# Products of two groups in a row, the first rows of x in two halves, and a new table of thresholds, in a planned attention kernel

## The chip, the cores and the metric

The kernel runs on one core of a Trainium2 chip. The metric is the time of one execution on the device in microseconds (us), as the median of several runs. One further execution was taken by the hardware profiler; its rows are what the argument rests on. The engines are PE (matmuls; PEld is its weight load), DVE (vector), ACT (activations), POOL, and SP, which here only issues DMAs.

## What is computed

Two attention layers over 2048 positions of width 512 with 32 heads of width 16; their outputs stand side by side.

```python
# A: softmax attention
scores = jnp.einsum("bhqd,bhkd->bhqk", q, k) * Dh ** -0.5
p = _softmax(scores, axis=-1)
o = jnp.einsum("bhqk,bhkd->bhqd", p, v)        # then @ wo
# B: linear attention with learned features
phi_q = concat([softmax(pq), softmax(-pq)]); phi_k = concat([softmax(pk), softmax(-pk)])
kv = jnp.einsum("bhsf,bhsd->bhfd", phi_k, v); z = jnp.einsum("bhsf->bhf", phi_k)
o = (phi_q @ kv) / (phi_q @ z + 1e-6)          # then @ wo
return jnp.concatenate([a, b], axis=-1)
```

Nearly all of the time goes to A: 32 heads times 2048 by 2048 scores.

## The kernel before, in words

**Work of layer A.** Four heads form a group, and there are eight groups. A unit is one group with 128 or 256 queries; there are 73 units. For every unit the scores are made twice. First with the queries on the partitions: PE writes tiles of 128 by 512 scores into banks of PSUM (L971), and DVE reduces them to the maximum of each row (L1084), one bank by one instruction (a single) or two neighbouring banks by one (a pair). The negated maxima go by POOL and two DMAs (in the last four units by DVE and PE) into a spare row of QZ, the masked copy of the queries. Then with the keys on the partitions: PE makes the scores again, with the maximum already subtracted (L1234), and ACT takes the exponential of one or two banks into the ring pT of 34 slots (L1246). Last the product: for each 512 scores of the four heads PE multiplies pT with V (L1324, in `pv_run`), with V's extra column of ones giving the sums. When a unit is done, its product is evacuated to X, divided, and later multiplied with the output weights (`oproj`, L1419). A few units (11) move part of the maxima to ACT (a Relu, L1011) and one DVE instruction (L1078).

**Work beside it.** Projections of Q, K and V (L696, L710, L777), turning x by matmuls with the identity (L807), and all of layer B are cut into "jobs". A job takes a bank, runs its matmuls in pieces, and leaves the bank when an evacuation (`evac`, L560 on ACT or L563 on DVE) has copied it out.

**The planner.** The order on every engine is fixed when the program is built. An account of costs (`_Account`) plays the execution: it holds a clock `K.now`, the time at which each engine is free, and ready tasks. ACT, DVE, POOL and SP are asked in this order whether they are free and take the ready task of the lowest priority number; evacuations stand ahead of reductions and exponentials. For PE, `pick_pe` decides what comes next: a score tile for DVE (`d_fill`), one for ACT (`e_fill`), a product (`pv_run`), a piece of a job, or filler matmuls that keep PE's share of use up (`fill_mm`, L1854; also repeated scores). It decides by the leads `sd` and `se`, the work in time that stands ready for DVE and ACT, and by thresholds that are set anew every 60 us of the account (`T.set` with a row of `TH` over the defaults `TH0`):

- COL, INCOL: how large the smaller lead must be before products or jobs run, and before PE leaves them;
- SINGLE, ESINGLE: the lead below which a single is filled where no pair of banks is free; DCAP, ECAP: the largest lead up to which scores are filled; DBIAS and ZBIAS: who is served first;
- UA, RF, REPM, LHARD, LHI: how much use of PE is kept up by fillers and repeats;
- PV_START, PV_LOW, PVN: at how many free ring slots or ready groups products are wanted;
- BAL: an evacuation may go to DVE only if the work left for DVE, by the account, exceeds that for ACT by no more than BAL.

**The start.** Six idle matmuls (L368) run while the loads come. x comes in blocks of 128 rows on SP's queue: blocks 0 and 1, 2 and 3, 4 to 7, then the V weights, blocks 8 to 11, the rest of the K weights, blocks 12 to 15, the rest of the Q weights; the first K and Q weights come on ACT's queue. Blocks 0 to 3 are turned by 16 matmuls into banks 0 to 3 (L374), two idle matmuls follow, and DVE and ACT copy two banks of 512 columns each (L381, L383). DVE also copies the first K and Q weights into a padded form (L361). Then K and Q of the first group are projected for 512 positions (L710), and `first_qz` makes QZ of units 0, 1 and 2 from the Q bank (L734). The account begins at 7.6 us.

Of the kernel before, what the change touches and what calls it, by code (L numbers as in the profile page):

```python
# [213 lines left out]
def bass_concat_heads__softmax_full_mha__linear_kernel_hedgehog__prompt_kernel(  # L214
# [21 lines left out]
    with contextlib.ExitStack() as es:  # L236
# [5 lines left out]
        P = _Plan()  # L242
# [85 lines left out]
        def load_x(name, b0, b1):  # L328
            t_xs[name] = P.dma("sp", dsem("xs%d" % name), lambda e: e.dma_start(
                xs[:, b0:b1, :], A_x[0][128 * b0:128 * b1, :].rearrange("(b p) n -> p b n", p=128)))  # L330
# [5 lines left out]
        load_x(2, 4, 8)  # L336
# [27 lines left out]
        t_wqp = pad_copy(WQp, 0, t_wq0)  # L364
# [5 lines left out]

        pe_idle(6, [t_zmv, t_ones])
        for rb in range(4):
            for ct in range(4):
                t_turn = P.op("pe", lambda e, rb=rb, ct=ct: e.matmul(  # L374
                    PS[:, ct, 128 * rb:128 * rb + 128], xs[:, rb, ct * 128:ct * 128 + 128], ident[:, :],
                    start=True, stop=True), [t_xs[rb // 2], t_ident] if ct == 0 else [])
        pe_idle(2)
        t_x0 = []
        for ct in range(4):
            if ct % 2 == 0:  # L380
                t_x0.append(P.op("dve", lambda e, ct=ct: e.tensor_copy(xAT[:, ct, 0:512], PS[:, ct, :]), [t_turn]))  # L381
            else:
                t_x0.append(P.op("act", lambda e, ct=ct: e.activation(  # L383
                    xAT[:, ct, 0:512], PS[:, ct, :], ACT.Copy), [t_turn]))
# [17 lines left out]
        for r in range(4):  # L402
# [8 lines left out]
            {'SINGLE': 1.013, 'ESINGLE': 1.026, 'ZBIAS': 0.274, 'DBIAS': 0.27, 'ZREST': 0.238},  # L411
            {'SINGLE': 0.647, 'UA': 0.441, 'RF': 0.465, 'REPM': 0.115, 'PV_LOW': 6, 'DCAP': 2.442, 'ZBIAS': 0.207, 'BAL': 68.611},
            {'SINGLE': 1.013, 'UA': 0.408, 'REPM': 0.215, 'LHI': 0.119, 'DCAP': 1.302, 'ECAP': 1.815, 'ZBIAS': 0.315, 'DBIAS': 0.27, 'BAL': -28.613},
            {'SINGLE': 1.157, 'UA': 0.408, 'RF': 0.436, 'REPM': 0.215, 'LHI': 0.03, 'PV_START': 5, 'PV_LOW': 5, 'DCAP': 1.302, 'ECAP': 1.815, 'ZBIAS': 0.315, 'BAL': -28.613},
            {'SINGLE': 0.287, 'UA': 0.425, 'RF': 0.532, 'REPM': 0.196, 'LHARD': 0.35, 'LHI': 0.119, 'DCAP': 1.302, 'ECAP': 1.815, 'ZBIAS': 0.315, 'DBIAS': 0.27, 'BAL': -27.419},
            {'SINGLE': 1.157, 'UA': 0.408, 'RF': 0.436, 'REPM': 0.214, 'LHARD': 0.383, 'LHI': 0.03, 'PV_START': 5, 'PV_LOW': 5, 'PVN': 3, 'DCAP': 1.322, 'ECAP': 1.904, 'ZBIAS': 0.315, 'BAL': -27.335},
            {'COL': 0.708, 'SINGLE': 1.157, 'UA': 0.441, 'REPM': 0.196, 'LHI': 0.065, 'PVN': 3, 'DCAP': 2.495, 'ECAP': 1.461, 'ZBIAS': 0.315, 'DBIAS': 0.27, 'BAL': -27.419},
            {'ESINGLE': 1.165, 'RF': 0.62, 'REPM': 0.196, 'LHI': 0.065, 'ECAP': 1.185, 'ZBIAS': 0.049, 'DBIAS': 0.27, 'BAL': -27.419, 'ZREST': -0.23},
            {'ESINGLE': 1.2, 'RF': 0.62, 'REPM': 0.196, 'LHI': 0.122, 'ECAP': 1.185, 'ZBIAS': 0.049, 'DBIAS': 0.27, 'BAL': -27.419, 'ZREST': -0.23},
            {'COL': 0.63, 'INCOL': 0.753, 'ESINGLE': 1.097, 'RF': 0.436, 'REPM': 0.196, 'LHI': 0.079, 'JOBHOLD': 20.274, 'DCAP': 2.036, 'ECAP': 1.185, 'ZBIAS': 0.034, 'DBIAS': 0.314, 'BAL': -27.419, 'ZREST': -0.23},  # L420
            {'COL': 0.487, 'INCOL': 0.753, 'SINGLE': 0.633, 'ESINGLE': 1.097, 'RF': 0.596, 'REPM': 0.196, 'LHI': 0.079, 'JOBHOLD': 20.274, 'DCAP': 2.036, 'ECAP': 1.185, 'ZBIAS': 0.034, 'DBIAS': 0.334, 'BAL': -27.419, 'ZREST': -0.23},
            {'COL': 0.63, 'INCOL': 0.753, 'SINGLE': 0.663, 'ESINGLE': 1.097, 'UA': 0.458, 'RF': 0.676, 'REPM': 0.196, 'LHARD': 0.355, 'LHI': 0.246, 'JOBHOLD': 14.826, 'PV_START': 5, 'DCAP': 2.036, 'ECAP': 1.276, 'ZBIAS': 0.072, 'DBIAS': 0.278, 'BAL': -30.019, 'ZREST': -0.23},
            {'COL': 0.53, 'INCOL': 0.753, 'SINGLE': 0.674, 'ESINGLE': 1.097, 'UA': 0.442, 'RF': 0.67, 'REPM': 0.369, 'LHARD': 0.317, 'LHI': 0.259, 'JOBHOLD': 12.459, 'PV_START': 5, 'DCAP': 2.021, 'ECAP': 1.276, 'ZBIAS': 0.129, 'DBIAS': 0.278, 'BAL': -37.649, 'ZREST': -0.23},
            {'COL': 0.35, 'INCOL': 0.753, 'SINGLE': 0.749, 'ESINGLE': 1.097, 'UA': 0.433, 'RF': 0.67, 'REPM': 0.369, 'LHI': 0.259, 'JOBHOLD': 25, 'PV_START': 5, 'ECAP': 1.276, 'ZBIAS': 0.391, 'DBIAS': 0.278, 'BAL': -37.649, 'ZREST': -0.23},
            {'COL': 0.53, 'INCOL': 0.753, 'SINGLE': 0.749, 'ESINGLE': 1.097, 'UA': 0.442, 'RF': 0.67, 'REPM': 0.369, 'LHI': 0.259, 'JOBHOLD': 17.436, 'PV_START': 5, 'ECAP': 1.276, 'ZBIAS': 0.129, 'DBIAS': 0.278, 'BAL': -37.649, 'ZREST': -0.23},
            {'COL': 0.486, 'INCOL': 0.753, 'SINGLE': 0.638, 'ESINGLE': 1.097, 'UA': 0.442, 'RF': 0.67, 'REPM': 0.348, 'LHI': 0.259, 'JOBHOLD': 17.436, 'PV_START': 5, 'ECAP': 1.276, 'ZBIAS': 0.129, 'DBIAS': 0.278, 'BAL': -30.554, 'ZREST': -0.23},
            {'COL': 0.486, 'INCOL': 0.753, 'SINGLE': 0.638, 'ESINGLE': 1.097, 'UA': 0.442, 'RF': 0.67, 'REPM': 0.189, 'LHI': 0.259, 'JOBHOLD': 17.436, 'PV_START': 5, 'ECAP': 1.276, 'ZBIAS': 0.129, 'DBIAS': 0.278, 'BAL': -30.554, 'ZREST': -0.23},
            {'COL': 0.486, 'INCOL': 0.753, 'SINGLE': 0.735, 'ESINGLE': 1.057, 'UA': 0.442, 'RF': 0.648, 'REPM': 0.21, 'LHI': 0.234, 'JOBHOLD': 17.436, 'DCAP': 2.479, 'ECAP': 1.276, 'ZBIAS': 0.129, 'DBIAS': 0.278, 'BAL': -37.429, 'ZREST': -0.23},
            {'COL': 0.657, 'INCOL': 0.753, 'SINGLE': 0.735, 'ESINGLE': 1.057, 'UA': 0.442, 'RF': 0.648, 'REPM': 0.21, 'LHI': 0.234, 'JOBHOLD': 13.418, 'DCAP': 2.479, 'ECAP': 1.171, 'ZBIAS': 0.129, 'DBIAS': 0.278, 'BAL': -30.554, 'ZREST': -0.23},
            {'COL': 0.486, 'INCOL': 0.753, 'SINGLE': 0.933, 'ESINGLE': 1.057, 'UA': 0.442, 'RF': 0.61, 'REPM': 0.21, 'LHARD': 0.251, 'LHI': 0.285, 'JOBHOLD': 17.436, 'DCAP': 2.479, 'ECAP': 1.356, 'ZBIAS': 0.119, 'DBIAS': 0.111, 'BAL': -37.429, 'ZREST': -0.23},  # L430
        ]
        T = _Thresholds()
        I32 = mybir.dt.int32
        K = _Account(P)
        K.now = 7.6
        T.set(TH0, TH[:1])
        for i in range(1, int(1200 / SEG)):
            K.at(i * SEG, lambda i=i: T.set(TH0, TH[i:i + 1]))
        for e in K.free:
            K.free[e] = 7.6  # L440
        K.free["pool"] = 14.0

# [1638 lines left out]
```

## Time and profile before

| | us |
|---|---|
| three runs | 1199.12, 1202.8, 1205.19 |
| median | 1202.8 |
| profiled execution, its own time | 1199.05 |
| its span, from the first instruction to the last | 1197.3 |
| granted clock of PE, mean of the span | 0.999 |

In the rows of the profile a group is given as line, engine, operation, written tile <- read tiles, shapes and count, then busy time (overlaps of its own instructions counted once), mean duration in ns, and idle time of the engine before it with what ended it. A row of the timeline gives start, length, and the same names, with like instructions in a row put together. A row of the stages gives the busy time and count of the engines in one stretch of time.

### The profile page before, as it was taken

How to read it: one execution, taken by the hardware profiler on the slowest of the kernel's cores; microseconds unless marked ns; L12 is line 12 of the kernel's file. 1: busy time of each engine (PE TensorE's matmuls, PEld its weight loads, DVE VectorE, ACT ScalarE, POOL GpSimd, SP SyncE). 2: the span in 40 equal slices, each digit the busy share in tenths (PEclk: the TensorE clock that was granted, in tenths of full speed). 3: DMA queues.
4: the chain of work that ended last, by engine and by line, in shares of the span. 5: the costliest groups of instructions: out<-in, count | busy, mean ns of one | idle time of the engine just before them, and what ended most of it. 6: DMA issues, size and time to landing. Idle time of an engine off the chain costs nothing.

```text
span 1197.3 us, 32106 instructions
## 1 busy us (share of the span) xinstructions
PE 1117.4 (93%) x13025; PEld 468.9 (39%) x13025; DVE 1170.3 (98%) x1290; ACT 1149.8 (96%) x1891; POOL 821.8 (69%) x1636
## 2 busy tenths in 40 slices
PE   8998999998999999999999998999999998899998
PEld 3433333343334333333433333333333333345555
DVE  8999999999999999999999999999999999999995
ACT  5898999999999999999999999999999999999997
POOL 8511211227888888888787887888888888888860
PEclk9999999999999999999999999999999999999999
DMA  5011221210002001001000101121112111111120
GB/s 142 9 25 43 42 48 32 43 38 8 8 14 35 8 6 26 13 10 22 12 7 17 25 7 22 22 49 31 29 34 33 35 34 27 20 29 37 33 30 18
DMA packets 104119, 33.61 MB, mean 28 GB/s; under 512 B 86692, under 2 KB 103972, under 8 KB 103972
## 3 DMA queue, kind: packets, MB, share of 16 engines
q1 hardware_dynamic: 102916, 31.31, 13.4%
q8 instruction: 102, 1.67, 0.6%
q14 instruction: 45, 0.37, 0.1%
q10 hardware_dynamic: 1056, 0.26, 0.1%
HBM read 5.26 MB, written 4.19 MB: 8 GB/s over the span
## 4 chain that ended last, share of the span: by engine, by line
ACT 38%; DVE 33%; PE 23%; SPq 2%; issue 1%; POOL 1%; DMA 1%
ACT pT L1246 32%; DVE part L1084 32%; PE PS L1234 7%; PE PS L971 6%; PE PS L1324 5%; PE PS L1419 2%; ACT eB L1639 1%; ACT xAT L560 1%; PE PS L777 1%; ACT zS L1011 1%; ACT X L560 1%; SPq L1392 1%; ACT WQp L560 1%; POOL uB L1588 1%; PE PS L1563 0%
## 5 line engine op out<-in xcount | busy, mean ns | idle before, releaser
L1084 DVE TENSOR_REDUCE part<-PS 128x2 f32<-128x1024 f32 (+1 forms) x1118 | 1130.0, 1079 | 7.6 <-PE PS L971 5.2
L1246 ACT ACTIVATE pT<-PS 128x512 bf16<-128x512 f32 (+1 forms) x1573 | 1027.7, 797 | 21.3 <-PE PS L1234 17.9
L1234 PE MATMUL PS<-QZ,KT 64*128 64x256 bf16 (+1 forms) x4906 | 560.4, 259 | 40.9 <-ACT pT L1246 22.0
L971 PE MATMUL PS<-KT,QZ 64*128 64x512 bf16 x2139 | 484.5, 383 | 26.3 <-DVE part L1084 9.7
L1234 PEld LDWEIGHTS PS<-QZ,KT 64*128 64x128 bf16 x4906 | 245.5, 94 | 323.1 <-ACT pT L1246 161.4
L971 PEld LDWEIGHTS PS<-KT,QZ 64*128 64x128 bf16 x2139 | 126.2, 93 | 198.2 <-DVE part L1084 72.2
L1324 PE MATMUL PS<-pT,VP 128*17 128x256 bf16 (+1 forms) x4672 | 186.7, 261 | 0.9
L1403 POOL TENSOR_TENSOR QT<-X,Yd 128x256 bf16<-128x256 f32 (+1 forms) x70 | 46.8, 668 | 95.4 <-DMA Yd<-Yd 95.1
L1324 PEld LDWEIGHTS PS<-pT,VP 128*17 128x17 bf16 x4672 | 74.9, 88 | 95.2 <-issue 79.0
L1588 POOL TENSOR_TENSOR uB<-uB 128x256 f32<-128x256 f32 (+2 forms) x160 | 83.4, 522 | 10.1
L1591 POOL TENSOR_SCALAR uB<-uB 128x256 f32<-128x256 f32 (+2 forms) x128 | 82.6, 646 | 11.2
L1116 POOL TENSOR_TENSOR dm<-part 128x16 f32<-128x16 f32 (+1 forms) x66 | 15.7, 238 | 91.1 <-DVE part L1084 90.8
L915 POOL TENSOR_TENSOR QZ<-QT,mask 128x512 bf16<-128x512 bf16 (+1 forms) x70 | 65.9, 941 | 15.7 <-PE PS L1234 12.8
L1645 POOL TENSOR_TENSOR xAT<-eB 128x512 f32<-128x512 bf16 x32 | 36.9, 1152 | 40.8 <-ACT eB L1639 40.6
L1677 POOL TENSOR_TENSOR wA<-eB,rB 128x1024 bf16<-128x1024 bf16 x32 | 61.7, 1928 | 2.0
L560 ACT ACTIVATE xAT<-PS 128x512 f32<-128x512 f32 (+3 forms) x83 | 50.1, 617 | 4.4 <-PE PS L1443 2.9
L1648 POOL TENSOR_TENSOR xAT<-xAT 128x256 f32<-128x256 f32 x64 | 36.0, 563 | 5.0
L1563 PE MATMUL PS<-WKp,xBT 128*128 128x512 bf16 x128 | 36.4, 383 | 1.1 <-ACT pT L1246 0.5
L1639 ACT ACTIVATE eB<-uB 128x1024 bf16<-128x1024 f32 x32 | 36.0, 1124 | 0.0
L1419 PE MATMUL PS<-WOp,QT 128*128 128x512 bf16 x120 | 35.8, 384 | 0.1
L1588 POOL TENSOR_TENSOR uB<-xAT,mB 128x512 f32<-128x512 f32 x32 | 33.8, 1057 | 1.8
L1662 POOL TENSOR_TENSOR WQp<-rB,WQp 128x64 f32<-128x64 f32 x96 | 30.6, 319 | 6.4
(113 smaller groups left out, 752.4 us busy)
## 6 DMA issues: line engine op xcount, KB each, us to landing
out_dram<-xAT SPq DMA_DIRECT2D x31, 128.0 KB, 1.8
Yd<-Yd SPq DMA_DIRECT2D x220, 16.0 KB, 2.1
QT<-eB SPq DMA_DIRECT2D x60, 32.0 KB, 2.0
QZ<-mcols SPq DMA_DIRECT2D x110, 1.0 KB
pT<-in_A_x_dram SPq DMA_DIRECT2D x3, 512.0 KB, 7.5
KT<-eB SPq DMA_DIRECT2D x48, 32.0 KB, 2.0
mcols<-stage SPq DMA_TRANSPOSE x69, 2.2
Yd<-Yd SPq DMA_DIRECT2D x60, 8.0 KB, 1.9
```

The lines of the kernel that those rows point to most:

```text
L560: return P.op("act", lambda e: e.activation(dst, src, ACT.Copy), tk)
L915: "pool", lambda e: e.tensor_tensor(QZ[:, u % NQZ, :, 0:w], QT[:, g, q0:q0 + w].unsqueeze(1).broadcast_to([128, 2, w]), mask2[:, 0, :].uns ...
L971: return e.matmul(PS[:, b, :], QZ[p:p + 64, u % NQZ, r % 2, qt * 128:qt * 128 + 128], KT[p:p + 64, g, kc * 512:(kc + 1) * 512], start=star ...
L1084: tk = P.op("dve", lambda e: e.tensor_reduce(o, banks_ap(banks), AX.X, ALU.max), dep)
L1234: tok = P.op("pe", lambda e, r=rs[k], b=banks[k], kt=kt, x=x: e.matmul(PS[:, b, x * w:(x + 1) * w], KT[64 * (r // 2):64 * (r // 2) + 64, g ...
L1246: tk = P.op("act", lambda e: e.activation(pT[:, s0:s0 + n, :] if n > 1 else pT[:, s0, :], banks_ap(banks), ACT.Exp, scale=0.25), dep)
L1324: tok = P.op("pe", lambda e, r=r, kt=kt, x=x, s=es_[r][1]: e.matmul(PS[32 * r:32 * r + 17, bank, 0:w], VP[:, kt, 4 * g + r, :], pT[:, s, x ...
L1419: return e.matmul(PS[:, b, :], QT[:, i, st * 128:(st + 1) * 128], WOp[:, i, :], start=(i == 0), stop=(i == 7))
L1588: return P.op("pool", lambda e: e.tensor_tensor(o, a, b, op), dep)
L1591: return P.op("pool", lambda e: e.tensor_scalar(o, o, 0.0, None, ALU.max), dep)
L1639: cx["e"] = K.task("act", (0.95, 1.07), lambda eng: P.op("act", lambda e: e.activation(eB[:], uB[:], ACT.Exp), toks(d3)), d3, prio=-0.5, n ...
L1677: cx["phi"] = K.task("pool", (1.95, 1.95 + PLAT), lambda eng: P.op("pool", lambda e: e.tensor_tensor(phiB[k].rearrange("p (g f) -> p g f", ...
```

## The change

It has three parts. **Products**: `pv_run` runs a ready group through `pv_one`, and if more than one group was ready and the next is of the same unit, it runs that one directly behind. **Start**: the first 512 rows of x are turned and copied in two halves of 256; Q of the first 256 positions is projected at once into bank 0, ahead of the account, so that QZ of units 0 and 1 doesn't wait for the rest; the padded Q weights are copied between the halves; two idle matmuls go; and the load of blocks 4 to 7 waits until blocks 0 and 1 have landed. The account begins at 6.8 us, with the early use of PE entered in it. **Thresholds**: all twenty rows of `TH` are other values; the defaults stay.

```diff
-        def load_x(name, b0, b1):
+        def load_x(name, b0, b1, dep=()):
...
-        load_x(2, 4, 8)
+        load_x(2, 4, 8, [t_xs[0]])
...
-        t_wqp = pad_copy(WQp, 0, t_wq0)
...
         pe_idle(6, [t_zmv, t_ones])
...
+        for hf in range(2):
+            for rb in range(2 * hf, 2 * hf + 2):
+                for ct in range(4):
+                    t_turn = P.op("pe", lambda e, rb=rb, ct=ct, hf=hf: e.matmul(
+                        PS[:, 4 * hf + ct, 128 * (rb % 2):128 * (rb % 2) + 128],
+                        xs[:, rb, ct * 128:ct * 128 + 128], ident[:, :],
+                        start=True, stop=True), [t_xs[hf], t_ident] if ct == 0 else [])
...
-        pe_idle(2)
...
+            if hf == 0:
+                t_wqp = pad_copy(WQp, 0, t_wq0)
         for ct in range(4):
+            t_q0 = P.op("pe", lambda e, ct=ct: e.matmul(
+                PS[:, 0, 0:256], WQp[:, ct, 0, :], xAT[:, ct, 0:256], start=(ct == 0), stop=(ct == 3)),
+                [t_wqp, t_x0[0, 2], t_x0[0, 3]] if ct == 0 else [])
...
-            {'SINGLE': 1.013, 'ESINGLE': 1.026, 'ZBIAS': 0.274, 'DBIAS': 0.27, 'ZREST': 0.238},
-            {'SINGLE': 0.647, 'UA': 0.441, 'RF': 0.465, 'REPM': 0.115, 'PV_LOW': 6, 'DCAP': 2.442, 'ZBIAS': 0.207, 'BAL': 68.611},
...
-            {'COL': 0.486, 'INCOL': 0.753, 'SINGLE': 0.933, 'ESINGLE': 1.057, 'UA': 0.442, 'RF': 0.61, 'REPM': 0.21, 'LHARD': 0.251, 'LHI': 0.285, 'JOBHOLD': 17.436, 'DCAP': 2.479, 'ECAP': 1.356, 'ZBIAS': 0.119, 'DBIAS': 0.111, 'BAL': -37.429, 'ZREST': -0.23},
+            {'COL': 1.005, 'ESINGLE': 0.908, 'UA': 0.445, 'RF': 0.477, 'JOBHOLD': 25, 'DCAP': 2.443, 'DBIAS': 0.361, 'BAL': 36.315},
+            {'COL': 0.977, 'ESINGLE': 1.111, 'UA': 0.445, 'RF': 0.477, 'REPM': 0.151, 'LHARD': 0.318, 'JOBHOLD': 25, 'DCAP': 2.676, 'ECAP': 1.319, 'ZBIAS': 0.221, 'DBIAS': 0.361, 'BAL': 36.315},
...
+            {'INCOL': 2.053, 'SINGLE': 0.273, 'ESINGLE': 1.009, 'LHI': 0.033, 'JOBHOLD': 25, 'ECAP': 2.6, 'ZBIAS': -0.016, 'BAL': 33.313, 'ZREST': 0.223},
...
-        K.now = 7.6
+        K.now = 6.8
...
         def pv_run():
+            u = pv_ready[0][0]
+            n = pv_count()
+            pv_one()
+            if n > 1 and pv_ready and pv_ready[0][0] == u:
+                pv_one(K.free["pe"])
+
+        def pv_one(after=None):
             u, j = pv_ready.pop(0)
```

The values that the prediction uses, by stage of 60 us (0 to 19):

| | before | after |
|---|---|---|
| SINGLE | 1.013, 0.647, 1.013, 1.157, 0.287, 1.157, 1.157, 0.619 x3, 0.633, 0.663, 0.674, 0.749 x2, 0.638 x2, 0.735 x2, 0.933 | 0.619 x5, 0.636, 0.416 x7, 0.563, 0.585, 0.619, 0.648, 0.273 x3 |
| BAL | 0, 68.6, then -37.6 to -27.3 | 36.3 x3, 35.6 x2, 46.5, 0, -8.2 x2, -31.3 x2, -24.3 x2, 33.3 x7 |
| COL | 0.795 x6, 0.708, 0.795 x2, then 0.35 to 0.657 | 1.005, 0.977 x5, 1.13, 1.111 x3, 1.122, 1.15 x2, 1.132 x2, 0.902, 0.795 x4 |

More of the change, by code (lines that the diff above doesn't have):

```diff
@@ L1328, in pv_run @@
             n = 2 if u >= NU - LASTU else 1
-            pe_start(pe_cost("col", n * MM), n * MM)
+            if after is None:
+                pe_start(pe_cost("col", n * MM), n * MM)
+            else:
+                area.append((after, n * MM, n * MM))
+                K.free["pe"] = after + n * MM
+                K.at(K.free["pe"], lambda: None)
             for _, s in es_:
```

95 lines of the change are left out of this document (49 added, 46 removed).

## The prediction

> **What bounds the kernel now.** I read the busy times first, then stages, then the durations of single forms, then the start.
>
> ```profile
> PE 1117.4 (93%) x13025; PEld 468.9 (39%) x13025; DVE 1170.3 (98%) x1290; ACT 1149.8 (96%) x1891; POOL 821.8 (69%) x1636
> ```
> ```profile
> 10.00:60.00 50.00, 49.35 (x432) 20.04 (x435) 49.48 (x52) 40.09 (x66) 35.32 (x39) 1.00 0.20 39
> 60.00:120.00 60.00, 52.81 (x649) 21.08 (x641) 57.95 (x62) 53.84 (x81) 10.53 (x26) 1.00 0.14 34
> ```
> ```profile
> 10.00:1180.00 1170.00, 1098.56 (x12609) 457.77 (x12608) 1161.06 (x1268) 1135.67 (x1875) 816.54 (x1625) 1.00 0.14 26
> ```
> ```profile
> 1180.00:1198.00 18.00, 12.10 (x377) 7.88 (x373) 4.98 (x10) 10.76 (x14) 0.46 (x1) 0.93 0.07 19
> ```
>
> The columns are PE, PEld, DVE, ACT, POOL busy, granted clock, DMA share, GB/s. From 10 to 1180 us DVE is busy 1161.06 of 1170: 8.9 us of idle in all. Before that DVE waits for its first scores, after it the last units drain. The span is therefore start (about 10) + DVE's stream (1170) + drain (17). PE and ACT stand high too, but what they wait for is not what ends the span. What DVE's stream is made of:
>
> ```profile
> L1084 DVE TENSOR_REDUCE part<-PS 128x2 f32<-128x1024 f32 x842 | 971.1, 1211 | 6.9 <-PE PS L971 4.8 <-PE PS L978 0.2
> L1084 DVE TENSOR_REDUCE part<-PS 128x1 f32<-128x512 f32 x276 | 177.7, 676 | 0.7 <-PE PS L971 0.5
> ```
> ```profile
> 480.28 5.75 DVE L1084 TENSOR_REDUCE part<-PS 128x2 f32<-128x1024 f32 x5 [0.16 <-PE PS L971]
> 1170.43 3.67 DVE L1084 TENSOR_REDUCE part<-PS 128x1 f32<-128x512 f32 x6
> ```
>
> 1960 tiles of 512 scores are reduced, 842 times two in one instruction (a pair) and 276 times one (a single). Instructions overlap at their ends, so the price of one more is the spacing of a run: a pair (5.75 − 1.211)/4 = 1.135 us, a single (3.67 − 0.676)/5 = 0.599. Two singles cost 2 × 0.599 − 1.135 = **0.063 us** more than a pair.
>
> ACT looks as full but is not: its runs of singles space closer than their durations.
>
> ```profile
> L1246 ACT ACTIVATE pT<-PS 128x512 bf16<-128x512 f32 x1098 | 614.9, 674 | 4.6 <-PE PS L1234 2.4
> 454.16 10.54 ACT L1246 ACTIVATE pT<-PS 128x512 bf16<-128x512 f32 x21
> ```
>
> (10.54 − 0.674)/20 = 0.493 us against a share of 614.9/1098 = 0.560 of busy time: up to 1098 × 0.067 = 74 us of ACT's busy time is overlap. Work moved from DVE to ACT would help, from ACT to DVE harms.
>
> **The change, part by part.** *The start.*
>
> ```profile
> 0.79 1.49 SPq L329 DMA_DIRECT2D pT<-in_A_x_dram  x3
> 5.47 0.62 PE L374 MATMUL PS<-ident,pT 128*128 128x128 bf16 x8 [0.59 <-DMA pT<-in_A_x_dram]
> 5.84 0.29 DVE L361 COPY WQp<-wA 128x512 bf16<-128x512 bf16 x1 [0.93 <-DMA wA<-in_A_wqkv_dram]
> 6.13 1.29 DVE L381 CAST xAT<-PS 128x512 bf16<-128x512 f32 x2
> 7.48 1.04 PE L710 MATMUL PS<-xAT,WKp 128*128 128x512 bf16 x4 [0.95 <-DVE xAT L381]
> 8.55 0.69 ACT L559 ACTIVATE KT<-PS,bias_k 128x512 bf16<-128x512 f32 x1 [1.34 <-PE PS L710]
> 9.42 1.35 DVE L734 TENSOR_TENSOR QZ<-PS,mask 128x256 bf16<-128x256 f32 x3 [2.00 <-PE PS L710]
> 10.69 5.74 DVE L1084 TENSOR_REDUCE part<-PS 128x2 f32<-128x1024 f32 x5
> ```
>
> Now the copies of the first 512 rows of x begin after the second half has landed and been turned (6.1), the K projection at 7.48, and Q stands behind it, so QZ begins at 9.42. Afterwards the first half's copies lie in the wait for the second half (5.47), and Q for 256 columns is projected before K. The second half is turned by 5.47 + 0.62 = 6.09; DVE copies the padded Q weights until 6.13, then two casts of half the width, taken at half of 1.29 us: 0.65, until 6.8. K then takes 6.85 to 7.9, its evacuation 0.69, to 8.6; QZ of the first units, on DVE from about 6.9 with its matmuls hidden behind the casts, is done meanwhile. From there the first reduction 0.8 later, at 9.4 (in the trace 10.69 − 9.42 = 1.27 us after QZ began, less a third of QZ's 1.35 for the first unit). That is **−1.3 us**. The new wait holds SP's queue: the load of x blocks 4 to 7 waits until blocks 0 and 1 have landed (4.2, when PE turned them) instead of going out by 2.3, and behind it stand the V weights, two more x loads and the other K and Q weights, all about 2 us later. Nobody in the trace is seen waiting for them; with four pairs (4.5 us) already fed by the first K chunk DVE has cover until 13.9, and the first loads meet less traffic. If the cover fails, the whole gain of 1.3 and up to 0.7 more is lost; if the first loads land earlier, up to 0.7 more is won: bounds −2.0 to +0.7.
>
> The two idle matmuls (0.59 us of PE) go too. Six others run first:
>
> ```profile
> 1.68 2.74 PE L368 MATMUL PS<-zmv,ones_t 128*128 128x512 bf16 x6 [1.68 <-POOL zmv L316]
> L368 PE MATMUL PS<-zmv,ones_t 128*128 128x512 bf16 x8 | 3.3, 567 | 1.7 <-POOL zmv L316 1.7
> ```
>
> They space (2.74 − 0.567)/5 = 0.435 us where the four of the K projection space (1.04 − 0.381)/3 = 0.22, though the granted clock reads 1.00 in all stages to 1180 us: the PE is slow first and fast by 7.5. [...] The turns and the Q projection now fill that place, so I take nothing.
>
> *Thresholds.* SINGLE is the lead of DVE under which a single is put in. By stage, the singles follow it:
>
> ```profile
> L1084 DVE TENSOR_REDUCE part<-PS 128x1 f32<-128x512 f32 x53 | 34.6, 676 | 0.0
> ...
> L1084 DVE TENSOR_REDUCE part<-PS 128x1 f32<-128x512 f32 x6 | 4.0, 679 | 0.0
> ...
> L1084 DVE TENSOR_REDUCE part<-PS 128x1 f32<-128x512 f32 x64 | 40.4, 676 | 0.0
> ...
> L1084 DVE TENSOR_REDUCE part<-PS 128x1 f32<-128x512 f32 x11 | 7.1, 683 | 0.0
> ...
> L1084 DVE TENSOR_REDUCE part<-PS 128x1 f32<-128x512 f32 x69 | 43.9, 674 | 0.2
> ```
>
> These are 120 to 240 us (SINGLE 1.013 and 1.157: 53), 240 to 300 (0.287: 6), 300 to 420 (1.157: 64), 420 to 600 (0.619: 11) and 1080 to 1198 (0.735 and 0.933: 69, the last units being narrow). The idle of DVE is no larger where singles are few: 59.81 busy of 60 in 240 to 300.
>
> ```profile
> 240.00:300.00 60.00, 54.95 (x613) 22.12 (x610) 59.81 (x61) 59.02 (x102) 28.42 (x59) 1.00 0.11 23
> ```
>
> The new table has 0.273 to 0.648 everywhere. By these rows ten stages at 0.56 to 0.65 would have 3.7 each, eight at 0.273 to 0.416 6 each, and the last two together 40 (an estimate, between 12 and 69): 125 in place of 276. 151 singles become 75 pairs: 75 × 0.063 = **−4.8 us**, between 0 and, with none left, 138 × 0.063 = −8.7.
>
> BAL is the difference of work left, DVE's less ACT's, up to which DVE may take an evacuation. It was negative in most stages and becomes +33 to +46 in 13 of 20 (0 to 360 and 780 to 1198), 0 in one. Those between 0 and 420 us and after 780:
>
> ```profile
> 0.00:420.00 420.00, 57.24 (x103) 1.00 0.16 35
> 780.00:1198.00 418.00, 45.82 (x92) 1.00 0.17 31
> ```
>
> 103 less the 16 of V, which only ACT takes, and 92: 179 that DVE would then be allowed. One stage of before had the permission, 60 to 120 us (BAL 68.6), with these evacuations on ACT and none on DVE:
>
> ```profile
> L560 ACT ACTIVATE eB<-PS 128x512 bf16<-128x512 f32 x5 | 3.0, 603 | 0.4 <-PE PS L777 0.2
> L560 ACT ACTIVATE X<-PS 128x256 f32<-128x256 f32 x3 | 1.1, 380 | 0.0
> L560 ACT ACTIVATE X<-PS 128x128 f32<-128x128 f32 x2 | 0.6, 321 | 0.0
> ```
>
> None of ten: ACT frees itself sooner and is asked first. I take 0, by this nearest row; none of ten still leaves room for one in four, 45 × about 0.5 us (between 0.3 and 0.6 by width) = +22 at the other end. ACT's relief buys nothing while DVE sets the pace.
>
> *Two groups in a row.*
>
> ```profile
> 601.92 0.61 PE L1324 MATMUL PS<-pT,VP 128*17 128x256 bf16 x16
> 603.00 0.40 PE L1324 MATMUL PS<-pT,VP 128*17 128x256 bf16 x8
> ```
>
> Two groups already follow each other at times (16 matmuls). The rule makes it usual: PE is away from scores 0.61 us at once instead of 0.40 twice, one change of mode fewer. PE is no bound, so this pays only through DVE's 8.9 us of idle, and costs only if DVE runs dry. COL, the lead both engines must have before products run, rises to cover it (0.35 to 0.8 before, 0.9 to 1.15 in the first sixteen stages after). I take 0, between −8.9 and +5 (one in ten of 256 double runs opening a gap of its extra 0.21 us).
>
> **Sum**: −1.3 − 4.8 = −6.1 us on the profiled execution, 1199.05 (span 1197.3): 1193.0. That execution is the equal of the lowest of the three shown (1199.12); their median is 1202.8, where the same saving gives 1196.7. Between the two I predict **1195**.
>
> **The rivals.**
>
> *DVE is given evacuations (slower).* BAL above zero makes DVE, which has no room, take what ACT was doing. For it: DVE's 98%, the sign of BAL, and a work difference near zero all along, since both engines end together. Against: none of ten. From one in eighth on (22 × 0.5 = 11) it eats the whole gain; at one in four +22, hence 1195 + 22 = 1217. Chance 0.24.
>
> *Nothing is left of it.* The pairs need two free neighbouring banks, and longer product runs keep banks and PE; DVE waits for pairs as long as it saves. For it: DVE's waits are all for score products (4.8 of 6.9 us). Against: the 240 to 300 us row. Then the start alone: 1200. Chance 0.2.
>
> *The idle goes too.* Fewer changes of mode let PE keep DVE fed; 8.9 us more at most: 1186. Chance 0.16.
>
> *The clock closes.* UA, the share of PE use that the filler matmuls keep up, falls a little in late stages (0.442 to 0.422). [...] All stages to 1180 read 1.00, so: over 1220, chance 0.05.
>
> **How the numbers follow.** The forecast has 0.35 (1190 to 1199). Range 1184 to 1217: it holds forecast, the lost gain, the closed idle and most of the evacuations. 0.5% of 1202.8, about what a measurement of this kernel can tell from no change, is 6 us: faster is under 1196.8, slower over 1208.8. Faster: 0.31 of the forecast and 0.15 of the closed idle, 0.46. Slower: 0.21 of the evacuations and 0.05 of the clock, 0.26. Within: 0.2 of the lost gain, 0.04 of the forecast, 0.03 of the evacuations and 0.01 of the idle, 0.28.
>
> **What would show it.** First reduction at 9.1 to 9.7 us; singles at or under 150, pairs over 900; DVE's evacuations (casts from PSUM) nought or few; DVE idle from 10 to 1180 us not over 9 us; product runs mostly of 16 matmuls; clock 1.00. It is wrong if DVE shows tens of casts from PSUM, if its idle for score products grows past 10 us, or if singles stay over 200.

## The result, and the profile after

The change made the kernel slower: 1208.79 us (median of eight runs, 1208.30 to 1211.62) against 1202.12 us for the kernel before (eight runs, 1198.66 to 1205.19); the ratio on record, which is not the quotient of the two medians (1.0055), is 1.0063, with a 95% interval of 1.0053 to 1.0073. The profiled executions are further apart, 1208.32 against 1199.05 (spans 1206.6 and 1197.3, so 9.3 us), because that of before lies at the fast end of its runs.

First the busy times of the changed kernel, and its row of the stages from 10 to 1180 us (PE, PEld, DVE, ACT, POOL, granted clock, DMA share, GB/s):

```profile
PE 1098.3 (91%) x13149; PEld 483.1 (40%) x13232; DVE 1180.1 (98%) x1255; ACT 1148.1 (95%) x1935; POOL 822.2 (68%) x1636
```
```profile
10.00:1180.00 1170.00, 1070.25 (x12527) 466.14 (x12607) 1161.41 (x1219) 1126.83 (x1905) 817.16 (x1625) 1.00 0.14 26
```

DVE idles 1170 − 1161.41 = 8.6 us there, as before (8.9), and the granted clock reads 1.00. So nothing starved: DVE was given more to do. Its start, and what its stream is made of:

```profile
7.04 0.74 DVE L747 TENSOR_TENSOR QZ<-PS,mask 128x256 bf16<-128x256 f32 x2
...
9.45 1.22 DVE L1099 TENSOR_REDUCE part<-PS 128x2 f32<-128x1024 f32 x1
10.59 1.28 DVE L573 CAST xAT<-PS 128x512 bf16<-128x512 f32 x2
```
```profile
L1099 DVE TENSOR_REDUCE part<-PS 128x2 f32<-128x1024 f32 x906 | 1044.0, 1212 | 6.6 <-PE PS L986 3.8
L1099 DVE TENSOR_REDUCE part<-PS 128x1 f32<-128x512 f32 x148 | 97.7, 679 | 1.7 <-PE PS L986 1.1
L573 DVE CAST xAT<-PS 128x512 bf16<-128x512 f32 x5 | 3.3, 680 | 0.0
L573 DVE CAST eB<-PS 128x512 bf16<-128x512 f32 x4 | 2.7, 681 | 0.0
L573 DVE COPY X<-PS 128x256 f32<-128x256 f32 x5 | 2.1, 415 | 0.0
L573 DVE COPY xAT<-PS 128x512 f32<-128x512 f32 x3 | 2.0, 680 | 0.0
L573 DVE COPY WQp<-PS 128x272 f32<-128x272 f32 x4 | 1.7, 424 | 0.0
L573 DVE COPY X<-PS 128x128 f32<-128x128 f32 x5 | 1.4, 285 | 0.1
L573 DVE CAST WKp<-PS 128x512 bf16<-128x512 f32 x1 | 0.7, 683 | 0.0
L573 DVE COPY xAT<-PS 128x272 f32<-128x272 f32 x1 | 0.4, 429 | 0.0
```

The first reduction starts at 9.45 instead of 10.69, and after that one reduction DVE turns to two evacuations: the rows of L573 (DVE's side of `evac`) count 28 of them between the first reduction and the last, where before had none. 27 of the 28 lie in stages whose BAL is above zero, one in the stage where it is 0, none where it is negative. In PE's timeline the product runs (256 columns) of 16 matmuls rose from some 67 to 171, and those of 8 fell from 268 to 25: the rule of two groups took effect. The reductions are 906 pairs and 148 singles, before 842 and 276. The last reductions of both kernels, the changed one first:

```profile
1186.09 2.35 DVE L1099 TENSOR_REDUCE part<-PS 128x2 f32<-128x1024 f32 x2
```
```profile
1179.03 1.88 DVE L1084 TENSOR_REDUCE part<-PS 128x1 f32<-128x512 f32 x3
```

They end at 1188.44 and 1180.91, which leaves 18.2 and 16.4 us of drain. With the prediction's spacings (an instruction overlaps its neighbour by 1.211 − 1.135 = 0.076 us; a pair saves 0.063), the 9.3 us between the profiles are then: start 9.45 − 10.69 = −1.2; the 28 evacuations, 14.5 us of durations less 28 × 0.076 of overlap, +12.3; 128 singles turned into 64 pairs, 64 × 0.063 = −4.0; drain +1.8. That makes +8.9; 0.4 remain for idle and small rows. This is where the time lies on DVE; whether DVE is the cause is another question, and the experiments answer it differently.

ACT's exponentials moved the other way, to more singles (1236 against 1098) and fewer pairs (406 against 475):

```profile
L1261 ACT ACTIVATE pT<-PS 128x512 bf16<-128x512 f32 x1236 | 687.5, 687 | 10.5 <-PE PS L1249 6.0 <-PE PS L986 1.4
L1261 ACT ACTIVATE pT<-PS 128x1024 bf16<-128x1024 f32 x406 | 432.8, 1085 | 15.5 <-PE PS L1249 13.8 <-PE PS L986 0.2
```

### The profile page after: what moved, and what is told of

It is laid out like the page before. It is cut to its first block, busy times and chain, and to the rows that moved or that the text cites. A ratio compares the mean times of both kernels' runs of the same rounds, so it can differ in the third digit from the quotient of the medians.

```text
span 1206.6 us, 32442 instructions
## 1 busy us (share of the span) xinstructions
PE 1098.3 (91%) x13149; PEld 483.1 (40%) x13232; DVE 1180.1 (98%) x1255; ACT 1148.1 (95%) x1935; POOL 822.2 (68%) x1636
## 4 chain that ended last, share of the span: by engine, by line
ACT 41%; DVE 32%; PE 25%; issue 2%; POOL 0%; DMA 0%; SPq 0%; POOLq 0%
ACT pT L1261 35%; DVE part L1099 30%; PE PS L1249 7%; PE PS L986 6%; PE PS L1346 6%; ACT xAT L570 1%; ACT eB L1666 1%; PE PS L1446 1%; PE PS L707 1%; DVE zS L1093 1%; ACT zS L1026 1%; ACT X L570 1%; PE PS L790 1%; ACT WQp L570 1%; PE PS L723 1%
## 5 line engine op out<-in xcount | busy, mean ns | idle before, releaser
L986 PE MATMUL PS<-KT,QZ 64*128 64x512 bf16 x2084 | 462.4, 383 | 29.6 <-DVE part L1099 11.8
L1249 PEld LDWEIGHTS PS<-QZ,KT 64*128 64x128 bf16 x4834 | 248.8, 94 | 317.2 <-ACT pT L1261 177.1
L986 PEld LDWEIGHTS PS<-KT,QZ 64*128 64x128 bf16 x2084 | 120.1, 93 | 204.9 <-DVE part L1099 82.7
L1346 PE MATMUL PS<-pT,VP 128*17 128x256 bf16 (+1 forms) x4672 | 160.3, 260 | 2.6 <-ACT pT L1261 0.7
L1346 PEld LDWEIGHTS PS<-pT,VP 128*17 128x17 bf16 x4672 | 86.8, 90 | 65.4 <-issue 44.1
L930 POOL TENSOR_TENSOR QZ<-QT,mask 128x512 bf16<-128x512 bf16 (+1 forms) x70 | 65.9, 941 | 17.5 <-PE PS L1249 8.5
L570 ACT ACTIVATE xAT<-PS 128x512 f32<-128x512 f32 (+3 forms) x75 | 45.8, 621 | 4.2 <-PE PS L1470 3.2
L1881 PE MATMUL PS<-zmv,ones_t 128*17 128x512 bf16 (+2 forms) x432 | 39.5, 377 | 7.2 <-DVE Yd L1383 1.1
L1615 POOL TENSOR_TENSOR uB<-mB,xAT 128x512 f32<-128x512 f32 x32 | 33.8, 1057 | 2.1
L1590 PE MATMUL PS<-WKp,xBT 128*128 128x512 bf16 x99 | 30.3, 381 | 5.4 <-issue 3.9
```

What stands on the lines that cost most here:

```text
L570: return P.op("act", lambda e: e.activation(dst, src, ACT.Copy), tk)
L930: "pool", lambda e: e.tensor_tensor(QZ[:, u % NQZ, :, 0:w], QT[:, g, q0:q0 + w].unsqueeze(1).broadcast_to([128, 2, w]), mask2[:, 0, :].uns ...
L986: return e.matmul(PS[:, b, :], QZ[p:p + 64, u % NQZ, r % 2, qt * 128:qt * 128 + 128], KT[p:p + 64, g, kc * 512:(kc + 1) * 512], start=star ...
L1249: tok = P.op("pe", lambda e, r=rs[k], b=banks[k], kt=kt, x=x: e.matmul(PS[:, b, x * w:(x + 1) * w], KT[64 * (r // 2):64 * (r // 2) + 64, g ...
L1346: tok = P.op("pe", lambda e, r=r, kt=kt, x=x, s=es_[r][1]: e.matmul(PS[32 * r:32 * r + 17, bank, 0:w], VP[:, kt, 4 * g + r, :], pT[:, s, x ...
L1615: return P.op("pool", lambda e: e.tensor_tensor(o, a, b, op), dep)
```

## The experiments

The first theory was the rival of the prediction: BAL above zero hands DVE 28 evacuations, DVE has no room, the time goes up by their length. Against it stood, first, that ACT is as full as DVE, and later, that the whole order counts and not one engine. All ratios are to the kernel before, run on the same chip, with 95% intervals; the changed kernel's is 1.0063. In the first two groups the order on every engine stays that of before or of the changed kernel (the account is told the old costs); in the third a new order is planned, but for a_nofill.

### Which engine's work costs time

**a_act** issues DVE's 28 evacuations on ACT, at their places in the changed order.

```diff
-                if eng == "act":
+                if eng == "act" or 10.0 < K.now < 1188.0:
```

> The changed kernel with its planned order kept, but the 28 evacuations that the plan gives to DVE between 10 and 1188 us are issued on ACT, at the same place in the order. Theory (DVE's work sets the pace): the 28 casts, 12.2 us of DVE's spacing by the trace, leave the stream, so the span falls by 8 to 12 us, to 1195 to 1199, about the kernel before. Rival (the order of PE and the banks sets the pace, the casts only fill holes): less than 3 us either way, 1204 to 1209.

Measured: 1215.61 us, 1.0123 [1.0106, 1.0139], 6.8 us **slower** than the changed kernel. Both expectations missed. The stages row and DVE's waits of a_act:

```profile
10.00:1180.00 1170.00, 1080.13 (x12526) 463.56 (x12528) 1147.91 (x1183) 1129.50 (x1924) 816.99 (x1624) 1.00 0.13 26
```
```profile
DVE part L1099 <- PE PS L986: 17.5, 44, 2.1
```

DVE's idle rose from 8.6 to 22.1 us, and its waits for score tiles from 4.9 us to 17.5. PE brings the tiles in a fixed order, and its waits for ACT's exponentials rose from 40.6 to 42.4 us; that what stands ahead of DVE's tiles now waits for ACT is my reading of the two. Relieving DVE at ACT's expense is a loss.

**b_dve** is the reverse: the order of before, every eighth flexible evacuation (29) on DVE. **b_xact** is before with 59 short copies added to ACT.

```diff
-                if eng == "act":
+                if eng == "act" and len(engs) > 1 and 10.0 < K.now < 1180.0:
+                    moved[0] += 1
+                if eng == "act" and not (len(engs) > 1 and 10.0 < K.now < 1180.0 and moved[0] % 8 == 4):
```
```diff
+            if extra[0] % 4 == 2 and 10.0 < K.now < 1180.0:
+                extra[1] = P.op("act", lambda e: e.activation(xt[:, :], zmv[:, 0:184], ACT.Copy), [t_zmv, extra[1]])
```

> The kernel before with its planned order kept, but every eighth evacuation that either engine may do (29 of them) is issued on DVE at its place in the order. Theory (DVE's work sets the pace): 29 casts of 0.3 to 0.6 us, about 12 us, go on top: 1209 to 1215. Rival (they fall into DVE's holes, and ACT is relieved): under 3 us.

> The kernel before with its planned order kept and 59 more small copies on ACT (184 columns from one tile on chip to another, about 0.21 us each, 12 us in all; they add nothing to the result). Theory (DVE sets the pace, ACT has room behind its 95% of busy time): under 3 us. Rival (ACT is as full as DVE, and any work on either costs its length): +8 to +12.

Measured: b_dve 1212.32, 1.0095 [1.0081, 1.0110]; b_xact 1209.70, 1.0079 [1.0060, 1.0098]. The evacuations on DVE went from 1.1 to 17.9 us of durations, and DVE's busy time, overlaps counted once, up by 13.4 (1170.3 to 1183.7); that cost 11.3 us, as the theory has it. But work given to ACT costs too, and the theory that ACT has room falls. The busy times of b_dve, and of b_xact with its added group:

```profile
PE 1118.1 (92%) x13025; PEld 468.9 (39%) x13025; DVE 1183.7 (98%) x1319; ACT 1145.4 (95%) x1862; POOL 822.0 (68%) x1636
```
```profile
PE 1119.2 (93%) x13025; PEld 469.3 (39%) x13025; DVE 1174.4 (97%) x1290; ACT 1161.9 (96%) x1950; POOL 821.9 (68%) x1636
L590 ACT ACTIVATE xt<-zmv 128x184 bf16<-128x184 bf16 x59 | 23.2, 393 | 0.0
```

The copies last 23.2 us in all, but they overlap their neighbours: ACT's busy time went from 1149.8 to 1161.9, up by 12.1, or 0.205 for a copy. That gave 8.6 us (1201.06, the median of before beside it, to 1209.70).

**a_short_dve** and **a_short_act** take work away in the changed order: on DVE 22 of the 28 evacuations, or on ACT every seventh flexible one (25), copy 16 columns only. **a_short_act2** does it to all flexible two-dimensional evacuations on ACT after 150 us (133 of them; folded weights and the last Y stay whole), **a_short_all2** to those on both engines, **b_short_act2** to the same ones of before. In all five the rest of the copied tile is stale.

```diff
+                if eng == "dve" and 70.0 < K.now < 1188.0 and name != "Wf":
+                    return P.op("dve", lambda e: e.tensor_copy(dst[:, 0:16], src[:, 0:16]), tk)
```
```diff
+                if 150.0 < K.now < 1188.0 and name not in ("Wf", "yB") and len(engs) > 1 and len(dst.shape) == 2:
+                    if eng == "act":
+                        return P.op("act", lambda e: e.activation(dst[:, 0:16], src[:, 0:16], ACT.Copy), tk)
```

> The changed kernel with its order kept; the evacuations that its plan gives to DVE after 70 us (23, but for the one of the folded weights) copy 16 columns of each tile instead of all, so part of the result's data is stale. About 8 us of DVE's work goes and ACT gets none of it. Theory (DVE's casts are what made the change slower): 6 to 8 us faster than the changed kernel, 1201 to 1203. Rival (the order, or ACT, sets the end): under 3 us faster, 1206 or more.

> The changed kernel with its order kept; every seventh evacuation that its plan gives to ACT after 70 us (of those that either engine may do) copies 16 columns of each tile instead of all, so part of the result's data is stale. About 7 us of ACT's work goes and DVE's is untouched. Theory (DVE alone sets the pace): under 2 us faster. Rival (both engines set it, since added work on ACT cost 8.6 us for 12): 3 to 6 us faster.

> The changed kernel in its own order, but after 150 us of the account every flexible two-dimensional evacuation (folded weights and the last Y apart) copies 16 columns only, on whichever engine it stands: some 115 on ACT (about 37 us of its time) and 18 on DVE (about 7 us) go, and what the copies should have written stays stale, so the result is not the reference's. Theory 'the whole order': each engine waits for the others in a fixed order and no one engine's work sets the time, so even 37 us less on ACT shorten the time by under 8 us (1201 to 1209). Rival 'ACT's work sets it since the change': 20 us or more faster (1190 or less).

> a_short_all2 without its part on DVE: the changed kernel in its own order, the same evacuations after 150 us shortened to 16 columns where they stand on ACT (133 of them, 44 us of ACT's busy time by a_short_all2's trace), DVE's 28 whole. What the copies should have written stays stale, so the result is not the reference's. a_short_dve alone gave 0.3 us and a_short_all2 8.1. Theory 'two engines take turns: DVE's stream is the floor, ACT's only sets where DVE waits': with DVE whole there is little idle left on DVE to close (8.6 us from 10 to 1180, of which a_short_act closed 0.8), so 1205 to 1208, a gain of 1 to 4 us. Rival 'ACT's evacuations gave all of it': 1202 or less.

> The kernel before in its own order with the same cut: every flexible evacuation after 150 us (all on ACT there) copies 16 columns only, the result stale. Theory as for a_short_act2: DVE's reductions are the floor of before as well, with 8.9 us of idle on DVE between 10 and 1180, so 1197 to 1201, a gain of 1 to 4 us for some 50 us less on ACT. Rival 'before is bound by ACT too': 8 us or more (1193 or less).

| | taken away | time | ratio |
|---|---|---|---|
| a_short_dve | 7.6 us of DVE | 1208.48 | 1.0056 [1.0043, 1.0069] |
| a_short_act | 7.4 us of ACT | 1207.46 | 1.0046 [1.0034, 1.0059] |
| a_short_act2 | 43.9 us of ACT | 1201.21 | 0.9997 [0.9987, 1.0008] |
| a_short_all2 | 43.9 us of ACT, 5.9 of DVE | 1200.67 | 0.9993 [0.9984, 1.0002] |
| b_short_act2 | 49.8 us of ACT in before | 1194.24 | 0.9939 [0.9922, 0.9955] |

What is taken away is the sum of the evacuations' durations on that engine, less the same sum in the experiment (on ACT 123.7 us in the changed kernel, 136.2 in before; on DVE 14.5). The rows of a_short_dve and a_short_act2 that say why, the stages and then DVE's waits of each:

```profile
10.00:1180.00 1170.00, 1069.09 (x12540) 466.46 (x12619) 1156.24 (x1219) 1127.38 (x1907) 817.22 (x1625) 1.00 0.13 26
```
```profile
DVE part L1101 <- PE PS L988: 8.9, 27, 0.7
```
```profile
10.00:1180.00 1170.00, 1079.57 (x12706) 466.51 (x12703) 1165.58 (x1229) 1107.10 (x1916) 817.24 (x1626) 1.00 0.14 27
```
```profile
DVE part L1102 <- PE PS L989: 2.2, 7, 0.6
```

And PE's two longest waits of the changed kernel and of a_short_act2:

```profile
PE PS L1249 <- ACT pT L1261: 24.7, 73, 0.6
PE PS L986 <- DVE part L1099: 11.8, 41, 0.7
```
```profile
PE PS L989 <- DVE part L1102: 31.0, 99, 0.7
PE PS L1252 <- ACT pT L1264: 17.2, 53, 0.6
```

With half of the time of DVE's evacuations gone (14.9 us to 7.3), the kernel's time went down by 0.3 us, which the intervals can't tell from none; DVE's idle grew from 8.6 to 13.8 and its waits for score tiles from 4.9 to 8.9 us, so the work taken away came back mostly as waiting, as the rival had it. With 43.9 us gone from ACT and DVE's work untouched, the kernel gained 7.6 us: DVE's idle fell by 4.2 to 4.4, and its busy time by 3.4 (1180.1 to 1176.7), since the same instructions ran closer together. PE, which had waited most for ACT's exponentials, now waited most for DVE; in before and b_short_act2 the same two waits go from 22.0 and 9.7 us to 13.7 and 31.1. My expectation for a_short_act2 (1 to 4 us, DVE's stream as the floor) missed; the rival, that ACT's part alone gives it, was right. a_short_act had pointed the other way: its 1.3 us lay under the 2 that the theory of DVE alone allowed, but by its interval they are not told from none either. a_short_all2 missed its range (1201 to 1209) by 0.3 us, and its rival, 20 us and more, fell: ACT's work counts, but a sixth of its durations (7.6 of 43.9). Before is no different: 7.2 of 49.8, between both expectations.

By the engine's busy time, overlaps counted once (the first row of each page), a microsecond **added** cost 0.8 on DVE (11.3 of 13.4) and 0.7 on ACT (8.6 of 12.1), and one **taken away** gave 0.05 on DVE (0.3 of 5.8) and 0.3 on ACT (7.6 of 27.4, 7.2 of 27.2). By durations ACT's figures are 0.4 and 0.14 to 0.17. Only ACT in before was tried both ways; DVE was loaded in one order and relieved in the other. A microsecond moved from DVE to ACT cost about a half (6.8 of 14.5 of durations). DVE at 98% is therefore not an independent bound. Its waits are for PE's score tiles; they grow when ACT alone is loaded (b_xact, 5.2 to 8.1), and in the changed order they shrink when ACT alone is relieved (a_short_act2, 4.9 to 2.2). The profiled execution of b_short_act2, at 1197.06 the slowest of its four, doesn't show this last (6.2 against 5.2). What holds a_short_all2, where DVE idles 8.1 us and ACT 63 of 1170, no run shows.

### The start

**b_halves** is before with the new start but for the early projection of Q (halves, the later copy of the Q weights, the load's wait, no idle matmuls, account as before). **b_late** is before with 26 idle matmuls in place of the two. **a_nodep** is the changed kernel without the wait of the third load.

```diff
-        pe_idle(2)
+        pe_idle(26)
```
```diff
-        load_x(2, 4, 8, [t_xs[0]])
+        load_x(2, 4, 8)
```

> The kernel before with its planned order kept and of the change only the turn and copy of the first 512 rows of x in two halves, the later copy of the Q weights, the wait of the third load of x, and no two idle matmuls (no early Q projection). Theory: K's projection starts at about 7.2 in place of 7.48, the first reduction some 0.3 us earlier than 10.69, and all of it reaches the end: -0.3 us, not to be told from none. Rival (the waiting loads come late and DVE runs dry within the first 30 us): +1 to +3 us.

> The kernel before with 26 idle matmuls in place of 2 between the turn of the first x and the K projection, planned order kept: the K projection waits until PE has done them, so the first reduction comes about 4 us later than 10.69. Theory (DVE's stream is without holes, what its start loses or wins reaches the end in full): +3 to +5 us, so the 1.2 us that the change wins at the start are worth about that at the end. Rival (the first 60 us have room and absorb it): under 1.5 us.

> The changed kernel without the wait of the third load of x for the first, planned order kept. Theory (the wait delays nothing that is needed, nor does it bring the first loads sooner): within 1 us of the changed kernel, 1208 to 1210. Rival (the loads behind it come late): 2 us or more faster.

Measured: b_halves 1201.82, 1.0001 [0.9992, 1.0011]; b_late 1205.85, 1.0032 [1.0019, 1.0045]; a_nodep 1208.60, 1.0056 [1.0043, 1.0068]. The first reductions of b_halves and b_late:

```profile
10.12 2.34 DVE L1088 TENSOR_REDUCE part<-PS 128x2 f32<-128x1024 f32 x2
```
```profile
15.57 4.61 DVE L1084 TENSOR_REDUCE part<-PS 128x2 f32<-128x1024 f32 x4
```

All three came as their theories said. In b_late the start came 4.9 us later, and 0.32% or 3.8 us of it reached the end. In b_halves it came 0.57 us sooner, which is below what the interval resolves (0.1% is 1.2 us); the early projection of Q, which brings the other 0.67 (10.12 to 9.45), has no run of its own. The load's wait makes no difference.

### The rule of two groups and the table

Here each kernel but a_nofill is planned anew. **b_pair** is before with the new `pv_run` alone, **a_nopair** the changed kernel with one group at a time, **a_thb** the changed code with the table of before, **a_nobal** the changed code with BAL at −40 in every stage. **a_tab** and **bp_tab** are the changed code and the code of b_pair with tables that I searched for by the planner's own account. **a_nofill** keeps the changed order and leaves the filler matmuls out.

```diff
-            if n > 1 and pv_ready and pv_ready[0][0] == u:
+            if False and n > 1 and pv_ready and pv_ready[0][0] == u:
```
```diff
-            for cq in range(4):
+            for cq in range(0):
```

> The kernel before with the product rule alone (two groups in a row); start and table as before, so the planner makes another order. Both theories expect it slower than before: by 5 us or more where the table misfits (1207 to 1230, with more idle on both engines); the rival, by which the rule itself costs, expects DVE's new idle to end at score products that stood behind runs of 16 product matmuls.

> The changed kernel with one group to a product run again; start and table as changed, so the planner makes another order. Theory (a table fits only the rules that it was found with; neither rule is worse by itself): slower than the changed kernel, by 5 us or more, 1214 to 1235. Rival (two groups in a row themselves cost the time, by keeping PE away from the scores): faster than the changed kernel, toward 1200.

> The changed kernel with the table of the kernel before, all else as changed. Theory 'a table fits only its own rules': 1225 to 1240, as in b_pair, where the same table met the same rule. Rival 'the new table is what costs': 1196 to 1203, the time of before or less.

> The changed kernel with BAL at -40 in every row, so that DVE takes no evacuation and the planner makes another order. Theory (DVE's casts are the loss, and the planner can do without them): faster than the changed kernel, toward 1198. Rival (the table holds for its own order only; any other order under it has more idle): slower than the changed kernel by 10 us or more, though DVE's work falls.

> The changed code with another table of thresholds (20 rows, all different from the changed kernel's), so with an order of its own. Theory 'the loss lies in the table, not in the rule of two groups': another table for the same rule comes out within a few us of the changed kernel, on either side of it, best at 1203 to 1207, as an account of the same planner says 1205. Rival 'the rule itself costs': no other table gets below 1209, and this one gives 1212 or more.

> The kernel before with the rule of two groups alone, as in b_pair (1227.55), but with a table made for that rule. Theory 'a table fits only its own rules': 1207 to 1212, some 17 us less than b_pair with the same rule. Rival 'the rule of two groups costs by itself': 1220 or more again.

> The changed kernel with its order kept, but without the filler matmuls that keep PE's share of use up (108 calls of four, where the kernel before has 25); the repeats of score tiles stay. Theory (no single engine's work is what made the change slower, the order is): under 2 us either way, 1207 to 1211, if the clock stays open. Rival one (the fillers stand in PE's way): 3 us or more faster. Rival two (the fillers hold the clock gate): a granted clock under 0.98 and 10 us or more slower.

| code | table | time | ratio |
|---|---|---|---|
| before | before | 1202.12 | 1 |
| before, new start without the early Q (b_halves) | before | 1201.82 | 1.0001 [0.9992, 1.0011] |
| before, two groups (b_pair) | before | 1227.55 | 1.0213 [1.0199, 1.0227] |
| before, two groups (bp_tab) | made for it | 1211.34 | 1.0076 [1.0061, 1.0091] |
| changed | changed | 1208.79 | 1.0063 [1.0053, 1.0073] |
| changed, one group (a_nopair) | changed | 1221.78 | 1.0162 [1.0146, 1.0177] |
| changed (a_thb) | before | 1230.38 | 1.0238 [1.0223, 1.0253] |
| changed (a_nobal) | changed, BAL −40 | 1234.25 | 1.0270 [1.0255, 1.0286] |
| changed (a_tab) | another | 1205.62 | 1.0030 [1.0019, 1.0042] |
| changed, no fillers (a_nofill) | changed | 1211.22 | 1.0088 [1.0069, 1.0107] |

Every pairing of one side's rule with the other side's table loses 13 us or more by the medians (12 by the ratios) against the kernel that the table belongs to, as expected, and a table made for the rule wins 16 of b_pair's 25 back. a_tab and bp_tab came as their theories said. What goes wrong where they don't fit shows in DVE's waits, here of b_pair and then of a_nobal (in before they were 5.2 us in 16 waits; in a_nopair they are 5.6, but there 38 evacuations went to DVE):

```profile
DVE part L1084 <- PE PS L971: 21.0, 40, 6.5
```
```profile
DVE lr L1411 <- DMA lr<-X: 11.1, 1, 11.1
...
DVE part L1099 <- PE PS L986: 28.4, 34, 6.8
```
```profile
10.00:1180.00 1170.00, 1056.62 (x12273) 452.21 (x12351) 1126.11 (x1146) 1110.84 (x1805) 812.20 (x1617) 1.00 0.13 26
```

With the rule of two groups DVE runs dry (21.0 us, one gap of 6.5). In a_nobal all 28 evacuations are off DVE and the pairs stay about as they are (912), yet DVE idles 1170 − 1126.11 = 43.9 us, and the two waits make most of it (the 11.1 us are one wait). The theory that the planner can do without them (toward 1198) fell, and the rival of a_nobal held. The permission of BAL is therefore no slip in this table: without it the rest of the table gives 25 us more. a_tab has 29 evacuations on DVE to the changed kernel's 28 and is 3.2 us faster, with an interval clear of the changed kernel's; its reductions:

```profile
L1099 DVE TENSOR_REDUCE part<-PS 128x2 f32<-128x1024 f32 x902 | 1039.7, 1213 | 7.1 <-PE PS L986 4.2
L1099 DVE TENSOR_REDUCE part<-PS 128x1 f32<-128x512 f32 x156 | 102.5, 680 | 1.7 <-PE PS L986 0.6 <-PE PS L1249 0.4
```

They are those of the changed kernel to within eight singles, so counts of pairs and singles don't carry the difference either.

a_nofill, 0.2 us beyond its range, gained nothing from leaving out work that computes nothing. Its six runs go with the granted clock, from 1208.84 at 0.999 and 1208.64 at 0.995 to 1215.95 at 0.989, where seven of the changed kernel's eight have 0.999 or 1.000. By its one run at 0.999 the 432 filler matmuls (39.6 us of PE) cost nothing, and without them the clock is mostly lower: neither rival came in its size, but the second has the direction. It is the only run that takes work from PE.

## Why the prediction was wrong

It said 1195 (range 1184 to 1217), faster; 1208.79 was measured. By its steps:

- **Start, −1.3**: measured −1.24 in the first reduction. Right in size, but partly by luck: the K projection began at 7.18 where 6.85 was reckoned, as the turns took 312 ns in the mean, against 223 in before (last section), and from the end of its evacuation to the first reduction went 0.50 (8.95 to 9.45) instead of 0.8. The wait on SP's queue costs nothing, as taken (a_nodep). K's own matmuls were no slower without the two idle ones: four took 1.04 us, as before.
- **Singles, 276 to 125, −4.8**: 148 were left, −4.0. Right in the sum (75 × 0.063 is 4.7, not 4.8), and the limits named for it (at or under 150 singles, over 900 pairs) held. The split was not right: the last two stages have 22 singles where 40 were reckoned, the others 126 where 85 were, and the two errors partly cancel.
- **Evacuations, "None of ten … I take 0, by this nearest row"**: this is the step that failed. 28 of the 179 permitted went to DVE, 1 in 6.4, past the point of one in eight from which the rival was to decide: 12.3 us against the 22 × 0.5 = 11 named there. One stage of before, 60 to 120 us, was no measure of twelve others: the planner asks which engine is free when an evacuation comes up, and in the changed order ACT has 69 more exponential instructions (that these are why DVE was so often the free one is argued, not shown). The prediction had the tell-tale (tens of casts on DVE), the price and the sign, and gave the case 0.24. The drain, which had no term, added 1.8.
- **"ACT looks as full but is not … Work moved from DVE to ACT would help", "ACT's relief buys nothing while DVE sets the pace"**: both wrong. a_act moved it and lost 6.8 us, b_xact added to ACT and lost 8.6, a_short_act2 relieved ACT and won 7.6 without touching DVE. The 74 us were a misreading: 1098 × 0.674 = 740 us of durations make 614.9 of busy time, so overlap was already out of it. What is left above 0.493 for each single arises where singles don't stand in a long run, and b_xact found no room in it.
- **"The span is therefore start + DVE's stream + drain"**: as a sum it holds, and it places the difference to 0.4 us. As a cause it doesn't: a_short_dve took 7.6 us out of that stream and gave back 0.3.
- **The clock, over 1220 (0.05)**: no run shows a stage with the clock closed, nor what that would cost. What the runs showed in its place: all stages of the changed kernel to 1180 us read 1.00, as those of before did, and the slowest run of a_nofill, at 0.989 the lowest clock of all runs, took 1215.95.
- **Two groups in a row, 0 (−8.9 to +5)**: too narrow. DVE's idle did stay at 8.6, so in the profile the term reads zero; but with the table of before the rule cost 25 us, and with the tables made for it +3.5 (a_tab against b_halves, by their ratios 0.29%, though b_halves lacks the early Q) and +9.1 (bp_tab against before, 0.76%).

The loss then belongs to rule and table together. The rule makes DVE run dry under the old table (b_pair); under the new table it doesn't, and DVE takes 28 evacuations. That the evacuations *replace* the waits is my reading of a_nobal and b_pair, not shown by itself, and a_short_dve says that they alone are not what costs the time. Left open is the price of the rule under the best possible table: none tried came down to before, and no version found here beats both kernels.

## What to carry to other kernels

In a fixed order where three engines stand above 90%, adding up one engine's work tells where a difference lies and not what would remove it: lengthening one of two full engines cost 0.7 to 0.8 of the busy time added, shortening it gave 0.05 to 0.3 of what was taken away. Compare engines by busy time with overlaps counted once on both, since durations alone halve ACT's price here. Judge a scheduling rule together with thresholds that were searched for it, since rule and table crossed cost 13 to 28 us here while the two fitted kernels differ by 7. When a permission changes from never to often, count what could use it and price the whole range from the first case that decides the sign; a zero from one stage of a kernel in which the other engine was free is not a zero.

## What the runs showed of the hardware

PE's fast pace began at different times behind the same matmuls. Both kernels run the same six idle matmuls from 1.68 us, and then 16 turns; the turns of the changed kernel and of before:

```profile
4.21 2.12 PE L376 MATMUL PS<-ident,pT 128*128 128x128 bf16 x16
```
```profile
4.24 0.65 PE L374 MATMUL PS<-ident,pT 128*128 128x128 bf16 x8
```

Before, eight turns spaced (0.65 − 0.223)/7 = 0.061 us from the start (mean duration 223 ns); in the changed kernel all 16 took 312 ns in the mean:

```profile
L376 PE MATMUL PS<-ident,pT 128*128 128x128 bf16 x16 | 2.1, 312 | 0.0
```

The weight loads of the second eight turns, in the changed kernel and in b_halves, and those of b_late's idle matmuls:

```profile
5.30 0.77 PEld L376 LDWEIGHTS PS<-ident,pT 128*128 128x128 bf16 x8 [0.30 <-DMA pT<-in_A_x_dram]
```
```profile
5.18 0.45 PEld L375 LDWEIGHTS PS<-ident,pT 128*128 128x128 bf16 x8 [0.18 <-DMA pT<-in_A_x_dram]
```
```profile
7.26 0.15 PEld L368 LDWEIGHTS PS<-zmv,ones_t 128*128 128x128 bf16 x1 [0.28 <-issue]
7.62 4.42 PEld L368 LDWEIGHTS PS<-zmv,ones_t 128*128 128x128 bf16 x21 [0.21 <-issue]
```

So the slow pace lasted until about 6.3 us in the changed kernel's execution and to about 5 in that of b_halves. In b_late it lasted past 7: the loads came 0.43 us apart to 7.26, then (4.42 − 0.15)/20 = 0.21. The same matmuls ran ahead in all four until 4.2 us. What sets the moment, from 4.2 us (before) to over 7 (b_late), was not shown.

A copy on ACT of 184 columns from on-chip memory (L590 above) took 393 ns (0.205 us of ACT's busy time, neighbours' overlap taken off), and the 133 cut ones of 16 columns in a_short_act2 207 ns in the mean (27.5 us in all), against 623 for 512 columns from PSUM: a short instruction is far from free. And the kernels differ in spread: eight runs of before lie 6.5 us apart, seven of eight of the changed kernel within 0.65.

The spread goes with the granted clock, a per mille at a time. The 74 runs of before that stood beside the experiments have clocks of 0.995 to 1.000; the eight at 1.000 took 1199.7 us in the mean, the seven at 0.996 took 1202.7. The changed kernel's slowest run, 1211.62, is the one at 0.996. At 0.999 before takes 1201.2 (11 runs) and the changed kernel 1208.6 (6 runs), so the loss is not the clock's.
